# Attention with head mixing, then two MLPs: a times v moved from six visits of a row group to two, and the second mixing moved ahead in the slot behind a visit

## The chip, the cores and the metric

The kernel runs on one core of a Trainium2 chip. The metric is the device time of one execution in microseconds (us); the median of several runs counts.

## The reference, cut to what matters

The kernel computes attention with two mixings over the heads, and then two MLPs on its output. The change is in the attention alone. There are 4 batches of 12 heads, 448 positions and 64 columns a head.

```
scores = scale * q @ k.T                                  # per batch and head, 448 x 448
scores = einsum('bhij,hg->bgij', scores, w_pre)           # first mixing over the heads
attn   = exp(scores - max) / (sum + 1e-9)                 # softmax over j
attn   = einsum('bhij,hg->bgij', attn, w_post)            # second mixing over the heads
out    = attn @ v                                         # "a times v"
x = out as [1792, 768];  x = ((x @ w1) * (x @ w2)) @ w3 @ w_out
x = relu(x @ w_in) ** 2 @ w_out2
```

## The kernel before, in words

**Row groups and blocks.** The 448 rows of a batch are cut in groups of 110, 110, 110 and 118 rows, so there are 16 row groups (s = 0 to 15). A group is cut into blocks of 10 rows times 12 heads, 120 partitions: 11 blocks, or 12 in the fourth group. `BLK` lists all 180 blocks, `first[s]` is the first block of group s.

**The slots.** The loop over `u` (line 1320) runs through 180 slots and six more, one a block. All instructions are put down by hand in this order, and each engine works through its own part of them in that order. In slot u:
- TensorE does the first mixing (`premix`, line 284, two matmul records each) of blocks u + 1 and u + 2 if u is odd, the second mixing (`postmix`, line 380, 12 matmuls) of block u - 4 (`LAG`), and at the end of the slot what is planned for it under `END`: scores (`qk`, line 241) and a times v (`av`, line 494).
- DVE (VectorE) does the row maximum of block u (line 298), every second slot the reciprocals, the low half of the split of E for even blocks (`EL`, line 367), and the low half of the second mixing's output of block u - 5 (`ATl`, line 402).
- ACT (ScalarE) does the high half of that output (`ATh`, line 396) first, then what is planned as `FIRST` (the copy of scores, `evict_s`, line 248, and the copy out of a times v, `put_xh`, line 513), then the exponential of block u (line 306).
- POOL (GpSimd) does the high half of the split of E (`EH`, line 353) and both steps of its low half for odd blocks (`F` and `EL`, lines 364 and 365).
- SP issues the regroup of block u + 5 (`Bt<-S`), after everything else of the slot.

**Work planned by slot.** The dictionary `events` holds, by slot, what comes beside the blocks, each with a kind that says where in the slot it stands (`LOAD`, `FIRST`, `MID`, `LOW`, `END`). A slot with scores or a times v is called a visit here. For group s the scores of the six pairs of heads are made in six visits (`qs`), at the offsets 0, 1, 3, 5, 7, 9 (0, 2, 4, 6, 8, 10 for a long group) from four slots before the first block of group s - 1. Each is six matmuls with 64 rows, in three pairs that run side by side on the two halves of the rows.

A times v of group s comes when all of the group's blocks have passed the second mixing. For each pair p of the six pairs of heads it has two parts of 12 matmuls with 64 output columns, pairs of which run side by side on the two halves of the columns. Before, line 597 finds the six visits of scores that come after group s is done, and puts one pair of heads into each, behind the scores there (line 605). Where there are not six such visits (the last groups), the offsets 0, 1, 3, 5, 6, 7 are used. Three pairs (`hg` 0 or 1) share one accumulator bank (`ps_a`, a pool of one); behind the third, ACT and DVE copy it out as two halves (`put_xh`, `put_xl`, one slot later), and SP stores these (`store_x`, another slot later). The last group is done apart, in pieces between slot 177 and the end.

**Banks.** First mixings have three PSUM banks, second mixings two, the scores one pair of banks, a times v one. A second mixing can start once ATl of the mixing two before has read its bank, and a first mixing once the exponential three blocks before has.

**Other planned work.** In three batches k and v are split into halves while the blocks run: `split_k` on DVE and `split_kl` on POOL every second slot from `ks` on (slots in `full` have ACT make EH of odd blocks instead of POOL); `split_v` on ACT two slots, `split_vl` on DVE one slot ahead of the a times v that needs them. `scale_v` finds the scale of v through two tiny matmuls, whose output lies in the bank of the previous group's a times v (line 445).

Of the kernel before, what the change touches and what calls it, by code (L numbers as in the profile page):

```python
# [18 lines left out]
P = 128  # L19
CP = 112  # L20
F64_BIAS = 2.0 ** -112
NR = 10
ROWS = (110, 110, 110, 118)
LEAD = 5
LAG = 4
EG = 7
EW = 66
TB = 4
# [6 lines left out]
def talking_heads_attention_moe_moe2(  # L35
# [16 lines left out]
    B, _, NDC, S = k.shape  # L52
# [38 lines left out]
    def psum(pool, tag, dt=F32):  # L91
        return pool.tile([P, 512], dt, tag=tag, name=tag)
# [346 lines left out]
    def scale_v(b, i):  # L439

        m = vsum[b]
        if i == 0:
            nc.vector.tensor_reduce(m[:CP, 6:7], m[:CP, 0:6], axis=AX.X, op=ALU.max)
        elif i == 1:
            t = pav[4 * b - 1, 1] if b else psum(ps_a, "a")
            vps[b] = pt = t[:, 512 - P :]
            nc.tensor.transpose(pt[:1, :CP], m[:CP, 6:7], ident[:CP, :CP])
        elif i == 2:
            nc.vector.tensor_reduce(m[:1, 7:8], vps[b][:1, :CP], axis=AX.X, op=ALU.max)
        elif i == 3:  # L450
            nc.tensor.matmul(vps[b][:, :1], ones[:1], m[:1, 7:8], start=True, stop=True)
        else:
            up, lo = pow2(vps.pop(b)[:, :1], 14, "vs")
            nc.vector.tensor_scalar(
                xs[:, b : b + 1], lo, wunscale, 2.0 ** XSH, op0=ALU.mult, op1=ALU.mult
            )
            Vsc[b] = up
# [91 lines left out]
    def at(slot, kind, f, *a):  # L549
        events.setdefault(slot, []).append((kind, len(events), f, a))  # L550

    low_k, crowded, copies = set(), set(), []
    for s in range(2, NSUP):
        b = SUP[s][0]
        base = first[s - 1]
        L = first[s] - base
        qs = [base - 4 + p * L // NDC for p in range(NDC)]
        made = list(qs)
        if s == 2:
            made[:3] = base - 5, base - 2, base - 1  # L560
        for p in range(NDC):
            at(made[p], END, qk, s, p)
            copies.append((base - 2 if s == 2 and p == 0 else made[p] + 1, s, p))
            if p % 3 == 0:
                at(qs[p] - 9, LOAD, load_q, s, p // 3)
                at(qs[p] - 5, MID, split_q, s, p // 3, None)
                if p == 0 and qs[p] - 4 in low_k:
                    crowded.add(qs[p] - 3)
                at(qs[p] - 4 + (qs[p] - 3 in crowded), LOW, split_ql, s, p // 3)
        if s % 4 == 0:  # L570
            ks = [(first[s - 2] + 4) // 2 * 2 + 2 * p for p in range(NDC)]
            full.update(range(ks[0], ks[-1] + 4))
            for p in range(NDC):
                assert ks[p] + 1 < qs[p]
                at(ks[p], MID, split_k, b, p, None)
                at(ks[p] + 1, LOW, split_kl, b, p)
                low_k.add(ks[p] + 1)
                at(ks[p] - 4, LOAD, load_k, b, p)
    for slot, s, p in copies:
        at(slot, MID if slot in crowded else FIRST, evict_s, s, p)  # L580
    for b in range(B):
        f = first[4 * b]
        for i, slot in ((0, 9), (2, 11), (4, 13)):
            at(f + slot, MID, scale_v, b, i)
        for hg in range(2):
            for i in range(3):
                if b or hg:
# [2 lines left out]
                if b == B - 1:  # L590
                    at(f + 3 * hg + i + 13, MID, split_v, b, hg, i)
                    at(f + 3 * hg + i + 14, LOW, split_vl, b, hg, i)
    qk_at = sorted(x for x in events if any(e[2] is qk for e in events[x]))
    for s in range(NSUP - 1):
        for p in range(NDC):
            lo = first[s + 1] + LAG + 1
            at_qk = [x for x in qk_at if lo <= x < lo + SUP[s + 1][3]]
            slot = at_qk[p] if len(at_qk) == NDC else lo + (0, 1, 3, 5, 6, 7)[p]
            if s % 4 == 0 and s < NSUP - 4:
                b = SUP[s][0]  # L600
                assert slot - 2 > first[s] + 13
                at(slot - 2, MID, split_v, b, *divmod(p, 3))
                at(slot - 1, LOW, split_vl, b, *divmod(p, 3))
            for part in range(2):
                at(slot, END, av, s, p, part)
            if p % 3 == 2:
                at(slot + 1, FIRST, put_xh, s, p // 3)
                at(slot + 1, MID, put_xl, s, p // 3)
                if s < NSUP - 2:
                    at(slot + 2, END, store_x, s, p // 3)  # L610

    for b in range(B):
        for i, slot in ((1, 10), (3, 12)):
            at(first[4 * b] + slot, END, scale_v, b, i)

    last = NSUP - 1
    for p in range(NDC):
        for part in range(2):
            at(first[last] + TB + LAG + 1 + (2 * p + part) * (NB - first[last] - TB) // 12,
               END, av, last, p, part, (0, TB * NR))  # L620


    order = ExitStack()
# [693 lines left out]

    mlp_start = first[NSUP - 1] - 4
    early = iter(())
    for u in range(NB + LAG + 2):  # L1320
        if u == NB - LEAD:
            limit[0] = len(chunks)
# [20 lines left out]
        do(LOAD)  # L1343
        if 0 <= u - LAG - 1 < NB - LAG:
            at_h(u - LAG - 1)
        if u in AHEAD:
            postmix(u - LAG)
        if u % 2:
            for x in (u + 1, u + 2):
# [14 lines left out]
                split_l(u - 2)  # L1364
        if 0 <= u - 3 < NB and not low_on_pool(u - 3):
            split_l(u - 3)
        if 0 <= u - LAG < NB and u not in AHEAD:
            postmix(u - LAG)
        if 0 <= u - LAG - 1 < NB - LAG:
            at_l(u - LAG - 1)  # L1370
# [1 line left out]
        do(LOW)  # L1372
        for eng, cost, f in islice(early, STEPS.get(u, 0)):
            f()
        do(END)
        if NB <= u < NB + LAG:
            assert next(early, None) is None
            allow[0] = place["w1", 2]
# [928 lines left out]
```

## Time and profile before

| | us |
|---|---|
| median of 3 runs (lowest, highest) | 1222.35 (1222.11, 1223.85) |
| the profiled execution | 1222.48 |
| its span, first to last instruction | 1220.8 |
| its mean granted TensorE clock | 1.000 |

Mean duration of one instruction, from the page's costliest groups: the row maximum (line 298) 0.612 us, the exponential (line 306) 0.645, ATh (line 396) 0.562, ATl (line 402) 0.645, EL on DVE (line 367) 0.921, EH on POOL (line 353) 0.751, EL on POOL (line 365) 1.162, one record of a first mixing (line 284) 0.560.

How to read it: times are of one profiled execution. A matmul's duration holds its way through the array, and matmuls overlap; what one costs the engine is the distance from its start to the start of the next. A row of the timeline has the start, the duration, the engine, the line, what is written and read, the shape and how many instructions it stands for; a bracket at its end is idle time of the engine before it and what ended it.

### The profile page before, as it was taken

The page shows a single profiled execution, that of the slowest core. Times are in us where ns is not written, and L with a number is a line of the kernel's source. Part 1 is how long each engine was busy: PE and PEld are TensorE (multiplying, and loading weights), DVE is VectorE, ACT ScalarE, POOL GpSimd, SP SyncE. Part 2 cuts the span into 40 slices and gives each one's busy share as a digit, 9 for nine tenths or more (in the row PEclk, how much of TensorE's full clock was granted, in tenths as well). Part 3 has the DMA queues.
Part 4 walks back from the last instruction along what each step waited for, and adds up shares of the span by engine and source line. Part 5 has one row for each costly group of instructions (what it writes and reads, how often), then busy time and mean ns, then how long its engine had stood idle before and what let it go on. Part 6 is the DMA issues. An engine that isn't in the chain of part 4 may idle for free.

```text
span 1220.8 us, 26222 instructions
## 1 busy us (share of the span) xinstructions
PE 1206.9 (99%) x9904; PEld 746.7 (61%) x9904; DVE 948.8 (78%) x1690; ACT 804.5 (66%) x1620; POOL 587.6 (48%) x569
## 2 busy tenths in 40 slices
PE   8999999999999999999999999999999999999998
PEld 3666676676676665555557985555555555666665
DVE  6988899888889956766675876697778775999773
ACT  6887888878888735654464545567878876654430
POOL 3898788889879510110001311446233424666340
PEclk9999999999999999999999999999999999999999
DMA  6466555655645843755543537344478659656562
GB/s 193 129 161 163 138 146 132 171 126 155 172 119 162 242 128 95 175 127 156 134 134 112 189 120 242 127 159 166 160 251 290 240 185 314 207 162 187 171 196 79
DMA packets 139843, 205.02 MB, mean 168 GB/s; under 512 B 33764, under 2 KB 114788, under 8 KB 139716
## 3 DMA queue, kind: packets, MB, share of 16 engines
q1 hardware_dynamic: 136020, 200.01, 55.4%
q10 hardware_dynamic: 3136, 2.40, 0.8%
q8 instruction: 78, 1.28, 0.4%
q0 software_dynamic: 560, 0.93, 0.4%
q14 instruction: 49, 0.40, 0.1%
HBM read 114.60 MB, written 50.16 MB: 135 GB/s over the span
## 4 chain that ended last, share of the span: by engine, by line
PE 90%; DMA 4%; DVE 3%; ACT 1%; issue 0%; SPq 0%; ACTq 0%; POOL 0%
PE mm L1248 25%; PE mm L2113 16%; PE mm L1861 16%; PE p L284 9%; PE o L380 7%; PE mm L1525 5%; PE s L241 5%; PE a L494 4%; DMA Bt<-S 2%; PE p L1248 2%; DVE ATl L402 1%; DMA x<-x_d 1%; DVE EL L367 1%; DVE st L298 1%; ACT E L306 0%; DMA vraw<-in_v_dram 0%
## 5 line engine op out<-in xcount | busy, mean ns | idle before, releaser
L1248 PE MATMUL mm<-x,w 128*128 128x448 f16 x1044 | 197.7, 352 | 0.0
L1248 PEld LDWEIGHTS <-w 128*128 128x128 f16 x1152 | 112.2, 98 | 105.2 <-issue 1.0
L1861 PE MATMUL mm<-x,wq 128*128 128x448 f16 x882 | 169.2, 352 | 0.0
L284 PE MATMUL p<-Bt,wpre_k 120*120 120x448 f32 x360 | 159.4, 560 | 5.7 <-DMA Bt<-S 3.1
L2113 PEld LDWEIGHTS <-ao 128*128 128x128 f16 x1176 | 115.0, 98 | 76.0
L380 PEld LDWEIGHTS <-EH 120*112 120x112 f16 (+1 forms) x1440 | 124.3, 130 | 44.6 <-issue 37.2
L353 POOL TENSOR_SCALAR EH<-E,st 120x448 f16<-120x448 f32 (+1 forms) x152 | 113.0, 751 | 47.7 <-DVE st L336 35.6
L1861 PEld LDWEIGHTS <-wq 128*128 128x128 f16 x882 | 86.0, 98 | 79.6
L402 DVE TENSOR_TENSOR ATl<-o,ATh 112x480 f16<-112x480 f32 x180 | 116.1, 645 | 23.9 <-ACT ATh L396 22.9
L396 ACT CAST ATh<-o 112x480 f16<-112x480 f32 x180 | 101.2, 562 | 45.7 <-PE o L380 40.7
L306 ACT ACTIVATE E<-p,st 120x448 f32<-120x448 f32 x180 | 116.1, 645 | 21.5 <-DVE st L298 13.1
L380 PE MATMUL o<-wph,EH 120*112 120x120 f16 x720 | 124.1, 219 | 1.2 <-DVE ATl L402 1.1
L380 PE MATMUL o<-wph,EL 120*112 120x120 f16 x720 | 122.0, 216 | 0.0
L380 PE MATMUL o<-wpl,EH 120*112 120x120 f16 x720 | 122.0, 216 | 0.0
L365 POOL TENSOR_TENSOR EL<-F,EH 120x448 f16<-120x448 f32 (+1 forms) x90 | 104.6, 1162 | 33.7 <-issue 20.4
L298 DVE TENSOR_REDUCE st<-p 120x1 f32<-120x448 f32 x180 | 110.2, 612 | 2.6 <-PE p L284 2.4
L1248 PE MATMUL mm<-h,M 128*128 128x448 f16 x576 | 110.2, 353 | 0.0
L2113 PE MATMUL mm<-x,ao 128*128 128x384 f16 x588 | 96.5, 326 | 0.0
L2113 PE MATMUL mm<-ow,ao 128*128 128x384 f16 x588 | 96.0, 326 | 0.0
L380 PEld LDWEIGHTS <-EL 120*112 120x112 f16 x720 | 93.6, 130 | 0.0
L367 DVE SCALAR_TENSOR_TENSOR EL<-E,st,EH 120x448 f16<-120x448 f32 (+1 forms) x90 | 82.9, 921 | 10.3 <-POOL EH L353 9.9
L1248 PEld LDWEIGHTS <-M 128*128 128x128 f16 x576 | 55.9, 98 | 52.0 <-DVE M L1435 0.8
(264 smaller groups left out, 2535.1 us busy)
## 6 DMA issues: line engine op xcount, KB each, us to landing
Bt<-S SPq DMA_DIRECT2D x176, 210.0 KB
raw<-in_moe_w_out_dram SPq DMA_DIRECT2D x24, 768.0 KB
g<-ev SPq DMA_DIRECT2D x64, 224.0 KB
gt<-g SPq DMA_DIRECT2D x56, 256.0 KB
raw<-in_moe_w_in_dram SPq DMA_DIRECT2D x16, 768.0 KB
raw<-in_moe_w_dram SPq DMA_DIRECT2D x14, 768.0 KB
raw<-in_moe_w_dram SPq DMA_DIRECT2D x16, 512.0 KB
kept_out<-xa SPq DMA_DIRECT2D x16, 384.0 KB
```

The costliest lines, as they stand in the source:

```text
L284: nc.tensor.matmul(pt[: n * H, :S], wpre_k.rearrange("p t g -> p (t g)")[: n * H, : n * H], Bt.pop(u)[: n * H], start=True, stop=True,)
L298: nc.vector.tensor_reduce(nsum[u][:n, 0, j : j + 1], Pp[u][:n, :S], axis=AX.X, op=ALU.max, negate=True)
L306: nc.scalar.activation(e[:n], Pp.pop(u)[:n, :S].rearrange("p (a b) -> p a b", a=EG), AF.Exp, bias=t[:n, 0, j : j + 1], scale=1.0, accum_ou ...
L353: nc.gpsimd.tensor_scalar(seven(EH[u][:n]), Ex[u][:n], inverse(u), 1.0, op0=ALU.mult, op1=ALU.mult)
L365: nc.gpsimd.tensor_tensor(a, f, b, op=ALU.subtract)
L367: nc.vector.scalar_tensor_tensor(a, e, inverse(u), b, op0=ALU.mult, op1=ALU.subtract)
L380: nc.tensor.matmul(pt[:CP, c * n : (c + 1) * n], a[:n, c * CP : (c + 1) * CP], w[:n, :n], start=(i == 0), stop=(i == 2),)
L396: nc.scalar.copy(ATs[s][0][:, :, :, m * NR : m * NR + nr], src)
L402: nc.vector.tensor_tensor(ATs[s][1][:, :, :, a], src, ATs[s][0][:, :, :, a], op=ALU.subtract)
L1248: nc.tensor.matmul(pt[:, :S], w[a][:, cs], x[z][:, sl], start=(c == 0 and i == 0), stop=(c == len(parts) - 1 and i == 2),)
L1861: nc.tensor.matmul(pt[:, :S], w[:, a, c * P : (c + 1) * P], xop(t, b, kb, c), start=(start and c == 0 and m == 0), stop=(c == 2 and m == 2 ...
L2113: nc.tensor.matmul(pt[:, :OH], y[:, a, q * P : (q + 1) * P], ow[g, q][kb][:, w], start=(start and q == 0 and m == 0), stop=(q == NQ - 1 an ...
```

## The change

A times v of groups 0 to 12 is put into two visits of scores instead of six: three pairs (`hg` 0) at the first visit, three (`hg` 1) at the fourth visit of group s + 3's scores, behind these scores (`END + 1`). Groups 13 and 14, which have no scores to go with, use the offsets 3 and 7. In a slot that follows a visit, the second mixing is issued ahead of the first mixings instead of behind them (`turned`). With it go some shifts: the splits of v stay one a slot and end two slots ahead of the run that needs them, the splits of k begin two slots earlier, `scale_v` has a bank of its own and goes one slot earlier for batches 1 to 3, and the kinds `END + 1` and `END + 2` order scores, a times v and the rest within the end of a slot.

```diff
@@ scale_v
         elif i == 1:
-            t = pav[4 * b - 1, 1] if b else psum(ps_a, "a")
-            vps[b] = pt = t[:, 512 - P :]
+            vps[b] = pt = psum(ps_a, "a")[:, 512 - P :]
@@ the planned work
+    double, from_pool = {}, {}
     for s in range(2, NSUP):
...
-        qs = [base - 4 + p * L // NDC for p in range(NDC)]
-        made = list(qs)
         if s == 2:
-            made[:3] = base - 5, base - 2, base - 1
+            qs = [base - 4 + p * L // NDC for p in range(NDC)]
+            made = [base - 5, base - 2, base - 1] + qs[3:]
+        else:
+            qs = made = [base - 4 + p * L // NDC for p in range(NDC)]
+            double[s] = qs[0], qs[3]
...
-            ks = [(first[s - 2] + 4) // 2 * 2 + 2 * p for p in range(NDC)]
+            ks = [(first[s - 2] + 2) // 2 * 2 + 2 * p for p in range(NDC)]
...
         for i, slot in ((0, 9), (2, 11), (4, 13)):
-            at(f + slot, MID, scale_v, b, i)
+            at(f + slot - (b > 0), MID, scale_v, b, i)
...
-    qk_at = sorted(x for x in events if any(e[2] is qk for e in events[x]))
     for s in range(NSUP - 1):
+        b, lo = SUP[s][0], first[s + 1] + LAG + 1
         for p in range(NDC):
-            lo = first[s + 1] + LAG + 1
-            at_qk = [x for x in qk_at if lo <= x < lo + SUP[s + 1][3]]
-            slot = at_qk[p] if len(at_qk) == NDC else lo + (0, 1, 3, 5, 6, 7)[p]
+            hg, i = divmod(p, 3)
+            slot = double[s + 3][hg] if s + 3 in double else lo + (3, 7)[hg]
             if s % 4 == 0 and s < NSUP - 4:
-                b = SUP[s][0]
-                assert slot - 2 > first[s] + 13
-                at(slot - 2, MID, split_v, b, *divmod(p, 3))
-                at(slot - 1, LOW, split_vl, b, *divmod(p, 3))
+                assert slot - 4 > first[s] + 13
+                at(slot - 4 + i, MID, split_v, b, hg, i)
+                at(slot - 3 + i, LOW, split_vl, b, hg, i)
             for part in range(2):
-                at(slot, END, av, s, p, part)
-            if p % 3 == 2:
-                at(slot + 1, FIRST, put_xh, s, p // 3)
-                at(slot + 1, MID, put_xl, s, p // 3)
+                at(slot, END + 1, av, s, p, part)
+            if i == 2:
+                at(slot + 1, FIRST, put_xh, s, hg)
+                at(slot + 1, MID, put_xl, s, hg)
                 if s < NSUP - 2:
-                    at(slot + 2, END, store_x, s, p // 3)
+                    at(slot + 2, END + 2, store_x, s, hg)
...
-            at(first[4 * b] + slot, END, scale_v, b, i)
+            at(first[4 * b] + slot - (b > 0), END + 2, scale_v, b, i)
...
-               END, av, last, p, part, (0, TB * NR))
+               END + 1, av, last, p, part, (0, TB * NR))
@@ the loop over the slots
+    turned = {x for x in events if any(y[2] in (qk, av) for y in events[x])}
...
-        if u in AHEAD:
+        if u in AHEAD or u - 1 in turned and 0 <= u - LAG < NB:
             postmix(u - LAG)
         if u % 2:
             for x in (u + 1, u + 2):
                 if x < NB:
                     premix(x)
...
-        if 0 <= u - LAG < NB and u not in AHEAD:
+        if 0 <= u - LAG < NB and u not in AHEAD and u - 1 not in turned:
             postmix(u - LAG)
...
-        do(END)
+        for kind in range(END, END + 3):
+            do(kind)
```

## Rows read from the trace of the kernel before

**Rows 1.** The page: busy time, share of the span and instructions of each engine.
```profile
PE 1206.9 (99%) x9904; PEld 746.7 (61%) x9904; DVE 948.8 (78%) x1690; ACT 804.5 (66%) x1620; POOL 587.6 (48%) x569
```

**Rows 2.** Windows: length, busy PE, PEld, DVE, ACT, POOL; clock, DMA share, GB/s.
```profile
260.00:285.00 25.00, 25.00 (x324) 17.23 (x323) 23.25 (x48) 21.67 (x48) 23.76 (x25) 1.00 0.57 149
...
360.00:385.00 25.00, 24.59 (x330) 17.31 (x330) 24.15 (x50) 20.95 (x45) 21.09 (x21) 1.00 0.60 169
...
408.00:430.00 22.00, 19.43 (x356) 14.63 (x355) 20.18 (x49) 16.80 (x37) 12.93 (x16) 1.00 0.97 277
```

**Rows 3.** Timeline, TensorE, two slots with one visit: start, duration, what.
```profile
289.27 0.22 PE L380 MATMUL o<-wph,EH 120*112 120x120 f16 x1
...
290.51 0.37 PE L241 MATMUL s<-kh,ql 64*110 64x448 f32 x2
...
290.81 0.24 PE L494 MATMUL a<-ATh,Vh 112*64 112x110 f16 x2
...
290.93 0.21 PE L494 MATMUL a<-ATh,Vl 112*64 112x110 f16 x2
...
291.37 0.21 PE L494 MATMUL a<-ATh,Vl 112*64 112x110 f16 x2
...
291.51 0.26 PE L380 MATMUL o<-wph,EH 120*112 120x120 f16 x1
...
292.13 0.22 PE L380 MATMUL o<-wph,EL 120*112 120x120 f16 x1
...
292.19 1.72 PE L284 MATMUL p<-Bt,wpre_k 120*120 120x448 f32 x4
...
293.74 0.22 PE L380 MATMUL o<-wph,EH 120*112 120x120 f16 x1
```

**Rows 4.** Timeline, TensorE, an early visit that has scores alone.
```profile
38.12 0.37 PE L241 MATMUL s<-kh,ql 64*110 64x448 f32 x2
38.43 0.26 PE L380 MATMUL o<-wph,EH 120*112 120x120 f16 x1
```

**Rows 5.** Timeline, TensorE, a times v alone between two second mixings.
```profile
396.60 0.22 PE L380 MATMUL o<-wph,EL 120*112 120x120 f16 x1
396.75 0.24 PE L494 MATMUL a<-ATh,Vh 112*64 112x110 f16 x2
...
397.45 0.26 PE L380 MATMUL o<-wph,EH 120*112 120x120 f16 x1
397.55 0.22 PE L380 MATMUL o<-wpl,EH 120*112 120x120 f16 x1
```

**Rows 6.** Timeline, TensorE: first mixings right behind a times v.
```profile
205.01 1.76 PE L284 MATMUL p<-Bt,wpre_k 120*120 120x448 f32 x4
```

**Rows 7.** Timeline, TensorE and DVE, slot 177 in the tail of the stage.
```profile
418.82 0.66 DVE L402 TENSOR_TENSOR ATl<-o,ATh 112x480 f16<-112x480 f32 x1 [0.70 <-ACT ATh L396]
...
420.38 1.99 PE L284 MATMUL p<-Bt,wpre_k 120*120 120x448 f32 x4 [0.85 <-ACT w L890]
...
422.20 0.22 PE L380 MATMUL o<-wph,EH 120*112 120x120 f16 x1
```

**Rows 8.** Timeline, other engines: copies of ACT, an F of POOL, an EL of DVE.
```profile
275.55 1.15 POOL L364 TENSOR_SCALAR F<-E,st 120x448 f32<-120x448 f32 x1
...
289.05 1.05 DVE L367 SCALAR_TENSOR_TENSOR EL<-E,st,EH 120x448 f16<-120x448 f32 x1 [1.11 <-POOL EH L353]
...
295.37 0.91 ACT L248 COPY S<-s 110x896 f32<-110x896 f32 x1 [0.23 <-PE s L241]
...
296.17 0.45 ACT L513 ACTIVATE xt<-a 128x330 f16<-128x330 f32 x1
```

**Rows 9.** Waits, 40 to 430 us: who waited for whom, us, times, longest.
```profile
DVE xt L522 <- ACT xt L513: 9.6, 15, 0.9
...
PE o L380 <- DVE ATl L402: 1.1, 3, 0.5
```

## The prediction, made before the change was run

> **What bounds the kernel now.** The page comes first: TensorE is busy 1206.9 of 1220.8 us [rows 1]. So the time is what TensorE does plus its few waits, and the change touches only the attention stage, some 450 us long. I then read that stage by windows [rows 2]. PE is full or nearly so in the first two of them, and after 408 us it loses 2.6 of 22 us to waits. The granted clock is 1.00 in each, the full one of its two levels (2.4 GHz), so no time is to be had from it. And the other engines are not far behind: DVE at 93 and 97%, ACT at 87 and 84%, POOL at 95% where v is split (260 to 285 us).
>
> Read closer, TensorE keeps a strict rhythm [rows 3]. A times v (line 494) steps by 0.049 us from one pair of matmuls to the next, second mixings (line 380) by 0.053 us from one to the next ((292.13 - 291.51) / 11 is 0.056 with a slow first step). Each change between shapes that use the array differently costs extra: from the third pair of scores to a times v 290.51 to 290.81, 0.30 us; from the last pair of a times v to the mixing 0.14, where 0.049 is the pace. Between second and first mixing nothing extra is paid: 292.13 to 292.19.
>
> **Fewer runs of a times v.** Before, each pair of heads makes its own run behind its own scores, six for each of 15 row groups (the last group is made in pieces). In [rows 3] a run lasts from 290.81 to 291.51, 0.70 us. Its inner pace is (291.37 - 290.93) / 9 = 0.049 us, so its 12 steps alone are 0.587 us, and 0.115 us is entering and leaving. What stands behind the scores does not matter: in [rows 4] scores without a times v reach a second mixing in 0.31 us (38.12 to 38.43), about what they pay to reach a times v. So a visit that loses its a times v saves 0.70 us, the run that receives it grows by 0.587, and 0.115 us is gained for each run that vanishes.
>
> How many vanish: row groups 0 to 12 have scores to follow (s + 3 up to 15), and six runs become two, 4 x 13 = 52: 6.0 us. Groups 13 and 14 have no scores beside them, but for the first visit of 13. A run alone between two second mixings [rows 5] costs 0.15 instead of 0.053 us to enter (396.60 to 396.75), 0.70 for itself (to 397.45), and 0.045 in the first step behind it (0.10 instead of 0.053): less 0.587 that is 0.255 us. Group 13 loses three such and one behind scores; group 14 loses two, since in its other slots the last group's a times v stands anyway. That is 5 x 0.255 + 0.115 = 1.4 us. Sum on TensorE: 7.4 us.
>
> **Second mixing first.** In a slot behind a visit the mixing now stands ahead of the two first mixings. The order itself costs TensorE nothing: the extra of the first step behind a times v is 0.045 us for either (a mixing 0.10 against 0.053 [rows 5]; the four matmuls of the first mixings span 1.76 us behind a times v [rows 6] and 1.72 behind a mixing [rows 3]), and between the mixings nothing is paid. One new neighbour arises, first mixing ahead of scores, about six times. No row shows it; the bounds are nothing and another 0.1 us, like the mixing's way to a times v in [rows 5], 0.6 us in all. I take nothing, since a full-array shape precedes the scores either way.
>
> What the order gives: ACT gets its cast of a mixing (line 396) 1.55 us earlier in an odd slot (292.19 to 293.74 [rows 3]) after a long visit. In the tail there is a measurable piece. The first mixing of slot 177 waits 0.85 us until 420.38 for ACT, which is held up by a weight cast, and the mixing of that slot comes after it, at 422.20 [rows 7]. It now stands ahead and fills 0.63 us of that hole. It can: the ATl that frees its bank ends at 419.48 (418.82 + 0.66 [rows 7]), and its EL was made by POOL a slot before that. I take 0.6 us, between nothing and 0.85.
>
> **What moves on the other queues.** The count of instructions and DMAs is unchanged: store_x still puts two on SP's queue one slot behind each copy out, ahead of that slot's regroup, now at other slots. The splits of v stay one a slot, four to two slots ahead of the run. Those of k (load on SP's queue, copy on DVE, low part on POOL) begin two slots earlier. scale_v gets its own bank and goes one slot earlier, where the previous group's first half has been copied out. None of it is on TensorE's path; I cost it at nothing beside the stalls below, which bound it.
>
> **What the rhythm costs.** This is the unknown. Before, two slots of TensorE last the same each time: from mixing 289.27 to 293.74, 4.47 us [rows 3]. After, two slots with scores alone last 4.47 - 0.70 = 3.77 us and two with a run of three 3.77 + 0.70 + 2 x 0.587 = 5.64 us; up to three of 3.77 follow each other. By their shares in the window of v's split [rows 2] the others need, in two slots, 4.47 x 23.25 / 25 = 4.16 us on DVE, 4.25 on POOL and 3.87 on ACT. A short pair of slots makes POOL fall 0.5 us behind, three of them 1.5; the long pair gives 1.4 back. It fits only just there, and with room elsewhere.
>
> The run also adds a wait. ACT's copy out of a times v (xt, line 513) is queued behind the copy of the scores (0.80 us, 295.37 to 296.17 [rows 8]) and now waits for all three pairs, 0.70 + 2 x 0.587 = 1.87 us from the scores' end. ACT stands for about 1 us, with an exponential and a cast behind it, and DVE's xt behind that, which already waited 9.6 us in 15 such places [rows 9]. One walk, with the means of the page's groups in the table above: scores start at 0, the run ends at 2.65, mixing A at 3.3, two first mixings at 4.85, mixing B at 5.5; then scores, and mixing C at 6.55. C takes A's bank, so A's low part (ATl) must be done by then. ACT: copy of scores to 1.7, xt from 2.8 to 3.1, an exponential to 3.8, at times EH to 4.4, the cast of A to 5.0; DVE's ATl to 5.65. The margin is 0.9 us, so there is no stall where nothing else is full.
>
> It is full in three stretches with v's split, where F takes 1.15 us on POOL [rows 8] and EH, of the same form, 0.75 on average; and in three with k's split DVE waits 1.11 us for POOL's EH ahead of an EL [rows 8]. I charge 0.7 us for each of the first, half of the 1.5 by which POOL falls behind, and 0.35 for each of the second, a third of that wait: 3.2 us. The ends are a gain of 1 us (PE's waits for ATl, 1.1 us in all [rows 9], go) and a loss of 13, below.
>
> The Trainium skill, "SBUF — State Buffer", section "Who interferes with whom", says that GpSimd and a VectorE instruction with two inputs in SBUF shut each other out for a whole instruction. The trace leans that way, as F's 1.15 us shows [rows 8]. By that rule one whole EL, 1.05 us there, could stand before POOL's next step at both runs of a stretch, 2.1 in place of 0.7 us three times: 1221.8, which lies in rival B.
>
> **Sum.** The profiled execution took 1222.48 us (span 1220.8 and 1.7 around it), 0.1 above the median of 1222.35. 1222.5 - 7.4 - 0.6 + 3.2 = 1217.7, against the median 1217.6.
>
> **Rivals.** A: no stall. For it the walk's margin, against it POOL's fill. 1222.4 - 8.0 = 1214.4, or 1213.4 if old waits go too. B: the heavy stretches swallow the gain. About seven of sixteen groups hold a split of k or v; if each loses its 0.46 us and half a microsecond to one more wait, 7 x 0.96 = 6.7 of 8.0 us are gone: 1221. For it POOL at 95% [rows 2]; against it the mean over such a group, 24.1 us of TensorE (4.47 x 5.5 less 0.46) and 23.4 of POOL (4.25 x 5.5). C, slower: ACT's queue decides. If in those seven groups the 0.95 us before xt is never made good, as ACT needs 3.87 us in two slots of 3.77, each of 14 runs costs it: 13.3 - 8.0 = +5, 1227.7. It decides once ATl comes 0.9 us later than in the walk. Against it: the long pair of slots gives ACT 1.8 us. That the change doesn't do what it says is not likely: the runs follow from the slots written out.
>
> **From cases to numbers.** The forecast's own case (1 to 5 us given back, 1215.4 to 1219.8) 0.56, A 0.10, B 0.22, C 0.12. Measurement tells a change from none beyond 0.2%, 2.4 us. Faster, under 1219.9: the forecast and A, 0.66. Same: B, 0.22. Slower: C, 0.12. The range leaves out the far ends of A and C: 1213.5 to 1222.8.
>
> **What would show it.** Runs of 72 matmuls on line 494 behind two of the six scores, each 1.87 us up to the mixing; scores reaching a mixing in 0.30 us; and PE's waits in the stage: few, with POOL or ATl before them in the v stretches if I am right, with ACT's xt before them if C is. PE should be through with the stage 5 us earlier. I am wrong if an added pair takes more than 0.59 us, or if PE waits over 5 us more between 50 and 408 us than before.

## The result, and the profile after

The changed kernel takes 1230.76 us (median of 4 runs, 1230.45 to 1233.65) against 1222.97 for the kernel before beside it: ratio 1.0069, 95% interval 1.0051 to 1.0086. It is slower by 7.8 us. Forecast were 1217.6 us, and the range ended at 1222.8.

The loss lies in the attention stage alone. The second mixing of the last block starts at 441.93 us before and at 450.02 after, and from there to the end of the span it is 778.8 and 779.0 us. Lines have moved: a times v is line 493 now, ACT's copy out 512, DVE's 521, the splits of v 465 and 472; 241, 248, 284, 306, 353, 364 to 367, 380, 396 and 402 are the same. The page: the row that answers to [rows 1], the shares of the chain of work that ended last, by engine, and one of the costliest groups (busy and mean, then the idle time before it and what ended most of it):

```profile
PE 1205.6 (98%) x9904; PEld 741.6 (60%) x9904; DVE 948.5 (77%) x1690; ACT 804.6 (65%) x1620; POOL 590.2 (48%) x569
...
PE 83%; DVE 8%; ACT 3%; DMA 3%; issue 1%; POOL 1%; SPq 0%; POOLq 0%; DVEq 0%
...
L380 PE MATMUL o<-wph,EH 120*112 120x120 f16 x720 | 127.4, 221 | 9.8 <-DVE ATl L402 8.5
```

The same chain and group before:

```profile
PE 90%; DMA 4%; DVE 3%; ACT 1%; issue 0%; SPq 0%; ACTq 0%; POOL 0%
...
L380 PE MATMUL o<-wph,EH 120*112 120x120 f16 x720 | 124.1, 219 | 1.2 <-DVE ATl L402 1.1
```

DVE's share of the chain is the news: 8% in place of 3, while TensorE's fell from 90 to 83%. The windows that answer to [rows 2], and one more:

```profile
260.00:285.00 25.00, 24.37 (x288) 15.91 (x288) 23.27 (x48) 20.82 (x46) 21.09 (x22) 1.00 0.53 137
360.00:385.00 25.00, 24.50 (x325) 16.94 (x323) 22.63 (x51) 21.07 (x47) 21.55 (x22) 1.00 0.54 143
408.00:430.00 22.00, 19.23 (x298) 14.44 (x297) 19.76 (x46) 17.31 (x41) 13.17 (x17) 1.00 0.90 246
185.00:210.00 25.00, 21.89 (x308) 15.45 (x307) 19.90 (x43) 18.30 (x41) 19.08 (x21) 1.00 0.52 133
```

In the last, where k is split, TensorE is idle for 3.1 of 25 us, and every other engine is less busy than TensorE: nothing is full on average, engines wait for each other in turn. Before, TensorE showed no idle time there:

```profile
185.00:210.00 25.00, 25.00 (x333) 17.72 (x333) 23.43 (x49) 20.89 (x47) 21.08 (x25) 1.00 0.54 137
```

TensorE's own work shrank as forecast. A run, from the third pair of scores to the mixing behind it:

```profile
297.61 0.38 PE L241 MATMUL s<-kh,ql 64*110 64x448 f32 x2
297.92 0.24 PE L493 MATMUL a<-ATh,Vh 112*64 112x110 f16 x2
...
299.79 0.26 PE L380 MATMUL o<-wph,EH 120*112 120x120 f16 x1
```

From its first matmul to that mixing it lasts 1.87 us (297.92 to 299.79), the forecast length. Waits I count as the time by which a step of TensorE from one record to the next exceeds its usual pitch, summed from 45 to 430 us. They were 6.0 us before and are 21.5 after. The stage is 8.1 us longer, so 15.5 - 8.1 = 7.4 us of TensorE's work are gone. The 21.5 us are mainly of two kinds.

**The exponential: 9.4 us** (6.7 at the wait and 2.7 in slower steps right behind, 26 places). TensorE, ACT and DVE after a visit with scores alone:

```profile
61.30 0.37 PE L241 MATMUL s<-kh,ql 64*118 64x448 f32 x2
...
61.60 0.26 PE L380 MATMUL o<-wph,EH 120*112 120x120 f16 x1
...
61.71 0.91 ACT L248 COPY S<-s 118x896 f32<-118x896 f32 x1 [1.00 <-PE s L241]
...
62.27 2.03 PE L284 MATMUL p<-Bt,wpre_k 120*120 120x448 f32 x4
...
62.51 0.64 ACT L306 ACTIVATE E<-p,st 120x448 f32<-120x448 f32 x1
...
63.29 0.28 PEld L284 LDWEIGHTS p<-Bt,wpre_k 120*120 120x120 f32 x2 [0.78 <-ACT E L306]
...
64.14 0.22 PE L380 MATMUL o<-wph,EH 120*112 120x120 f16 x1
```

The four records of the first mixings span 2.03 us instead of 1.72 [rows 3]: the second of the two waits for the bank that the exponential three blocks before frees. The exponential is queued on ACT behind the copy of the scores. ACT stands idle for 1.00 us until the scores are there, copies for 0.80 and then needs 0.6 for the exponential, until about 63.1. TensorE has only the mixing and one first mixing to do meanwhile. Before, the a times v behind the scores filled 0.70 us [rows 3], and ACT's two instructions fitted in. The places bear this out: 24 of the 26 lie right behind a visit with scores alone, two in the tail, and none behind one of the 21 visits with a run. In the list of waits below the copy of the scores has 3.3 us and the exponential 26.7: only the order of the rows shows that the copy stands ahead of the exponential.

**ATl: 10.6 us** (14 places, half of them between 1.0 and 1.2 us). POOL, then DVE, then TensorE, around a mixing that waits:

```profile
303.83 1.43 POOL L226 TENSOR_TENSOR ql<-qraw,qh 128x330 fp32r<-128x330 f32 x1
305.22 1.14 POOL L196 TENSOR_TENSOR kl<-kraw,kh 128x448 fp32r<-128x448 f32 x1
306.33 0.65 POOL L353 TENSOR_SCALAR EH<-E,st 120x448 f16<-120x448 f32 x1
```

```profile
307.01 1.05 DVE L367 SCALAR_TENSOR_TENSOR EL<-E,st,EH 120x448 f16<-120x448 f32 x1 [1.96 <-POOL EH L353]
307.98 0.65 DVE L402 TENSOR_TENSOR ATl<-o,ATh 112x480 f16<-112x480 f32 x1
```

```profile
308.68 0.21 PE L380 MATMUL o<-wph,EH 120*112 120x120 f16 x1 [1.02 <-DVE ATl L402]
```

POOL works without a gap through two low halves and EH; DVE's EL waits 1.96 us for that EH, ATl stands behind EL on DVE, and the mixing waits for ATl. The same chain stood in the kernel before, at the same place of the batch (POOL, DVE, TensorE):

```profile
295.52 1.52 POOL L226 TENSOR_TENSOR ql<-qraw,qh 128x330 fp32r<-128x330 f32 x1
297.00 1.13 POOL L196 TENSOR_TENSOR kl<-kraw,kh 128x448 fp32r<-128x448 f32 x1
298.11 0.64 POOL L353 TENSOR_SCALAR EH<-E,st 120x448 f16<-120x448 f32 x1
```

```profile
298.79 1.05 DVE L367 SCALAR_TENSOR_TENSOR EL<-E,st,EH 120x448 f16<-120x448 f32 x1 [1.10 <-POOL EH L353]
299.76 0.64 DVE L402 TENSOR_TENSOR ATl<-o,ATh 112x480 f16<-112x480 f32 x1
```

```profile
300.46 0.21 PE L380 MATMUL o<-wph,EH 120*112 120x120 f16 x1
```

There the EL waited 1.10 us and the mixing was 0.05 us late, since a times v filled 0.70 us ahead of it. A wait that DVE could afford before is one that TensorE pays for now. The waits of after, 40 to 430 us, answer to [rows 9] (who waited for whom: us, times, longest; PEld is the weight load and runs ahead of PE, so not all of its wait is lost: of the 26.7 us, 6.7 show as waits of TensorE):

```profile
PEld p L284 <- ACT E L306: 26.7, 42, 1.4
DVE xt L521 <- ACT xt L512: 19.4, 21, 1.9
...
ACT xt L512 <- PE a L493: 17.6, 22, 1.3
...
DVE EL L367 <- POOL EH L353: 12.4, 12, 2.0
...
PE o L380 <- DVE ATl L402: 8.5, 12, 1.1
...
PEld p L284 <- ACT S L248: 3.3, 17, 0.2
```

and in the kernel before, beside the two of [rows 9]:

```profile
PEld p L284 <- ACT E L306: 15.0, 38, 0.9
...
DVE EL L367 <- POOL EH L353: 8.8, 9, 1.1
ACT S L248 <- PE s L241: 6.8, 29, 0.3
```

ACT's xt does wait for the runs, 17.6 us in all, as the prediction had it; whether that is what TensorE pays for, the trace alone can't say.

### The profile page after: what moved, and what is told of

It reads as the page before. It is cut to its first block, busy times and chain, and to the rows that moved or that the text cites. A ratio compares the mean times of both kernels' runs of the same rounds, so it can differ in the third digit from the quotient of the medians.

```text
span 1229.0 us, 26252 instructions
## 1 busy us (share of the span) xinstructions
PE 1205.6 (98%) x9904; PEld 741.6 (60%) x9904; DVE 948.5 (77%) x1690; ACT 804.6 (65%) x1620; POOL 590.2 (48%) x569
## 4 chain that ended last, share of the span: by engine, by line
PE 83%; DVE 8%; ACT 3%; DMA 3%; issue 1%; POOL 1%; SPq 0%; POOLq 0%; DVEq 0%
PE mm L1248 25%; PE mm L2115 16%; PE mm L1863 16%; PE p L284 6%; PE o L380 6%; PE mm L1527 5%; PE a L493 4%; PE s L241 3%; DVE ATl L402 2%; DMA Bt<-S 2%; DVE EL L367 2%; PE p L1248 2%; DVE st L298 2%; ACT E L306 2%; DVE Vl L472 1%
## 5 line engine op out<-in xcount | busy, mean ns | idle before, releaser
L284 PE MATMUL p<-Bt,wpre_k 120*120 120x448 f32 x360 | 162.8, 560 | 6.9 <-DMA Bt<-S 4.3
L380 PE MATMUL o<-wph,EH 120*112 120x120 f16 x720 | 127.4, 221 | 9.8 <-DVE ATl L402 8.5
L402 DVE TENSOR_TENSOR ATl<-o,ATh 112x480 f16<-112x480 f32 x180 | 115.8, 644 | 13.9 <-ACT ATh L396 12.5
L365 POOL TENSOR_TENSOR EL<-F,EH 120x448 f16<-120x448 f32 (+1 forms) x90 | 98.5, 1095 | 38.2 <-issue 23.6
L396 ACT CAST ATh<-o 112x480 f16<-112x480 f32 x180 | 101.5, 564 | 12.2 <-PE o L380 10.6
L367 DVE SCALAR_TENSOR_TENSOR EL<-E,st,EH 120x448 f16<-120x448 f32 (+1 forms) x90 | 82.9, 921 | 13.9 <-POOL EH L353 13.6
L248 ACT COPY S<-s 110x896 f32<-110x896 f32 (+1 forms) x88 | 80.4, 914 | 17.7 <-PE s L241 15.4
```

The costliest lines, as they stand in the source:

```text
L284: nc.tensor.matmul(pt[: n * H, :S], wpre_k.rearrange("p t g -> p (t g)")[: n * H, : n * H], Bt.pop(u)[: n * H], start=True, stop=True,)
L365: nc.gpsimd.tensor_tensor(a, f, b, op=ALU.subtract)
L367: nc.vector.scalar_tensor_tensor(a, e, inverse(u), b, op0=ALU.mult, op1=ALU.subtract)
L380: nc.tensor.matmul(pt[:CP, c * n : (c + 1) * n], a[:n, c * CP : (c + 1) * CP], w[:n, :n], start=(i == 0), stop=(i == 2),)
L396: nc.scalar.copy(ATs[s][0][:, :, :, m * NR : m * NR + nr], src)
L402: nc.vector.tensor_tensor(ATs[s][1][:, :, :, a], src, ATs[s][0][:, :, :, a], op=ALU.subtract)
```

## The experiments

Times are ratios to the kernel before on the same chip, with 95% intervals; "the changed kernel" is the one above, at 1.0069. Where an expectation names a theory by letter or number, it says what it claims. Four mattered: T1, the copy out of a run on ACT's queue (rival C); T3, the turned order; load, that the splits and low halves on POOL and DVE are too much for the short slots (T2; T4 where k's splits alone are meant); and T5, which I formed only after the first runs, that a times v had covered ACT's copy of the scores.

**Each part alone.** e1 takes the turned order out of the changed kernel, e2 puts it alone into the kernel before.

```diff
-    turned = {x for x in events if any(y[2] in (qk, av) for y in events[x])}
+    turned = set()
```

> The changed kernel with the second mixing put back behind the first mixings everywhere; a times v stays in runs of three. Three theories of the 15.5 us by which TensorE's waits in the attention stage grew (6.0 to 21.5 us between 45 and 430 us): T1, the wait of ACT and DVE for the copy out behind a run of three (17.6 and 19.4 us of their time); T2, the uneven rhythm: pairs of slots that hold scores alone are now shorter (3.77 us) than ACT, DVE and POOL can follow, whatever the copy out does; T3, the order: the first mixings come 0.63 us later in a slot behind a visit, and the maxima and exponentials with them. T1: 1230 to 1234 us. T2: 1228 to 1234 us. T3: 1218 to 1222 us, the 7.4 us of saved changes without the waits.

> The kernel before with the second mixing first in the slot behind a visit, and nothing else of the change; six runs of a times v a row group. T1 and T2: within 1.5 us of before, 1221.5 to 1224.5. T3: 1230 us or more.

e1: 1232.66 us, 1.0087 [1.0070, 1.0104], 22.6 us of waits. e2: 1223.12 us, 1.0001 [0.9989, 1.0012]. Both lie where T1 and T2 put them, and T3 is out: the order costs nothing by itself and is not the cause. What is left of the change is the cause: the runs and the shifts that go with them.

**The copy out one slot later** (e3, in the changed kernel):

```diff
-                at(slot + 1, FIRST, put_xh, s, hg)
-                at(slot + 1, MID, put_xl, s, hg)
+                at(slot + 2, FIRST, put_xh, s, hg)
+                at(slot + 2, MID, put_xl, s, hg)
```

> The changed kernel with the copy out of a times v (ACT's high half, DVE's low half and the stores) one slot later, so that neither ACT nor DVE stands in front of it while the run of three is under way. T1: most of the 15.5 us of waits go, 1217 to 1221 us. T2 and T3: 1228 to 1232 us, though ACT's and DVE's own waits for the copy out fall from 17.6 and 19.4 us to under 5.

1239.45 us, 1.0144 [1.0128, 1.0159]: slower still, and outside both ranges. Its waits, 40 to 430 us:

```profile
ACT ATh L396 <- PE o L380: 26.8, 33, 1.4
PEld p L284 <- ACT E L306: 25.0, 31, 2.4
...
DVE xt L521 <- ACT xt L512: 9.4, 8, 1.4
...
PE o L380 <- DVE ATl L402: 8.6, 14, 1.3
```

ACT's wait for the runs is gone from the list and DVE's xt waits half as long, but TensorE's two kinds of wait are still there, 22.1 us in all against 20.0. T1 falls as the cause of them: ACT's wait in front of xt was there, but TensorE's waits did not go with it. Most of the rest of the 8.7 us over the changed kernel is the later copy itself and the tail: a matmul of scale_v waited 1.37 us for DVE's xt at two places, and in the tail TensorE stood 3.0 us for ACT's EH, up to 431.20, with a mean granted clock of 0.66 from 430 to 440 us, part of it at the lower of its two levels (1.00 in the changed kernel).

**Shorter runs** (e4): the six pairs in four visits, 2, 1, 2, 1.

```diff
-            double[s] = qs[0], qs[3]
+            double[s] = qs
...
+            qv = double.get(s + 3)
+            slot = (qv[0], qv[3])[hg] if qv else lo + (3, 7)[hg]
+            if qv and i == 2:
+                slot = (qv[2], qv[4])[hg]
```

> The changed kernel with a times v of groups 0 to 12 in four visits (two pairs, one, two, one at the scores' first, third, fourth and fifth visit), so two runs a group vanish instead of four (26 x 0.115 = 3.0 us in place of 6.0), and the copy out follows a run of one pair; scale_v takes its place in the bank of the previous group's first half. T1: the waits of before, less 3 to 4.4 us: 1218.5 to 1221 us. T2: short pairs of slots are rarer and are followed by longer ones sooner, about half of the added waits: 1223 to 1228 us. T3: 1229 us or more.

1233.10 us, 1.0092 [1.0077, 1.0107], some 20 us of waits, slower than T1 or T2 forecast (T3's range, but e2 has put T3 out). Halving the runs that vanish does not halve the waits. Visits without a times v remain, two a group in place of four; that these suffice is argued and not shown: by the list of waits the weight loads' wait for the exponential fell from 26.7 to 22.3 us, and the mixings' wait for ATl did not (8.5 and 9.1).

**The splits of k.** e5 gives the changed kernel the old slots of the split, e6 the kernel before the new ones (one line, + 2 against + 4; e5's edit is shown, e6's is its reverse). The slots in which ACT makes EH of odd blocks move with them:

```diff
-            ks = [(first[s - 2] + 2) // 2 * 2 + 2 * p for p in range(NDC)]
+            ks = [(first[s - 2] + 4) // 2 * 2 + 2 * p for p in range(NDC)]
```

> The changed kernel with the splits of k in their old slots (two later). So far the order alone cost nothing (1223.1), runs without it cost 1232.7, the copy out a slot later 1239.5, shorter runs 1233.1, so T1 and T3 in their plain form are out. T2, starvation and short pairs: TensorE gives nothing to ACT, DVE and POOL for as long as a long visit lasts, and these, loaded at 80 to 95%, cannot catch up in the short pairs that follow, most of all where k is split. T4: the splits of k at their new place collide with the visits (the group from 180 to 210 us alone lost 5.8 us). T2: 1228 to 1233 us. T4: 1220 to 1225 us.

> The kernel before with the splits of k two slots earlier, and nothing else of the change. T2: within 2 us of before, 1220.5 to 1224.5. T4: 1227 us or more.

e5: 1229.33 us, 1.0062 [1.0042, 1.0082], in T2's range, and against 1.0069 no difference that the intervals allow to tell. e6: 1227.56 us, 1.0045 [1.0030, 1.0060], in T4's range; its waits are 10.9 us, 3.5 of them in group 6, and those for ATl grow from 1.8 to 4.3. So the shift, which the prediction cost at nothing, costs 5.6 us alone, but given back to the changed kernel it returns about 1 (spans of 1228.0 and 1229.0 us). So the two costs don't add. That both are lateness of the same chain would explain it; no run shows it.

**Less work on DVE and POOL.** e7 (changed) and e8 (before) write only 4 of the 7 parts of EL and F and 2 of the 4 chunks of ATl; the high halves stand in for what is not written, and TensorE's matmuls are the same in number and shape.

```diff
+        e = e[:, :4]
...
-            ATs[s][1][:, :, :, a], src, ATs[s][0][:, :, :, a], op=ALU.subtract
+            ATs[s][1][:, :2, :, a], src[:, :2], ATs[s][0][:, :2, :, a], op=ALU.subtract
```

> The changed kernel with less work beside TensorE: EL is made for 4 of 7 parts of its columns only (on DVE and POOL, F too), ATl for 2 of 4 chunks, and TensorE reads the high halves in place of the parts left out, so its own matmuls are the same in number and shape. DVE loses about 1 us in two slots, POOL 0.7. T2: the waits go, and this is the changed kernel's TensorE time: 1213 to 1217 us, 4 to 8 us under the kernel before with the same relief. If the added waits are of another kind (the copy out, DMAs, SP's queue), it stays at 1226 us or more.

> The kernel before with the same relief, as a control. T2 and T4: its waits outside the tail are 3 us, so 1218 to 1222 us. If TensorE were slowed by something that the relief removes from its own stream, it would fall further.

e7: 1223.03 us, 1.0007 [0.9998, 1.0016]; e8: 1218.87 us, 0.9969 [0.9959, 0.9980]. e8 came as forecast; e7 fell between its two forecasts, so neither holds alone. The waits are 14.8 us against 3.1. In e7 ATl's fall from 10.6 to 2.5 us, those around the exponential stay: 6.5 and 3.2. So load makes the one kind and not the other, and with it gone the change still costs 4.2 us: 11.7 us more of waits, less the 7.4 saved. T5 came from here.

**Which engine makes ATl late.** e17 relieves DVE alone (its EL and ATl), e18 POOL alone (F and EL).

> The changed kernel with VectorE alone relieved: of ATl it writes 2 of the 4 chunks (the high halves stand in for the rest), of its EL 4 of 7 parts; GpSimd keeps all its EL, and TensorE's matmuls are the same in number and shape. Theory D (the second mixings wait for ATl because VectorE is too full): the waits for ATl fall from 10.6 us to under 4, and the time goes to 1223 to 1226. Rival P (VectorE is late because GpSimd's EL and the release of EH behind it are late): ATl's waits stay above 7 us and the time is 1228 to 1231. By both the waits for the exponential stay at about 9 us.

> The changed kernel with GpSimd alone relieved: its F and EL for the odd blocks write 4 of the 7 parts (high halves stand in for the rest); VectorE keeps all its work, and TensorE's matmuls are the same in number and shape. Theory D (VectorE is too full): ATl's waits stay above 7 us and the time is 1228 to 1231. Rival P (GpSimd's EL is late and VectorE waits for it): ATl's waits fall under 4 us and the time goes to 1223 to 1226. By both the waits for the exponential stay at about 9 us.

e17: 1224.86 us, 1.0026 [1.0016, 1.0035]; e18: 1227.79 us, 1.0046 [1.0029, 1.0063]. ATl's waits are 3.0 and 6.9 us by my count. By the list of waits, e17:

```profile
DVE EL L369 <- POOL EH L353: 13.5, 14, 2.0
...
PE o L382 <- DVE ATl L404: 2.2, 5, 1.0
```

and e18:

```profile
DVE EL L369 <- POOL EH L353: 8.6, 8, 2.0
...
PE o L382 <- DVE ATl L404: 4.7, 9, 1.3
```

e17 came as theory D had it. Rival P falls in its plain form: relieving F and EL on POOL did not bring ATl's waits under 4 us. But theory D missed e18's bounds too, by 0.1 and 0.2 us, and e17 leaves DVE's wait for POOL's EH as it was (13.5 us against 12.4). The chain runs through both engines, EL behind POOL's EH and ATl behind EL, and a relief of either shortens the waits, DVE's by more; the place at 308.68, 1.09 us late, was 0.26 late in e17 and 0.81 in e18. What stands ahead of EH on POOL there, the low halves of q and k, no run shortened.

**Without its cover, in the kernel before** (e14): the scores behind a times v instead of ahead of it, in all visits from group 3 on; no runs.

```diff
-            at(made[p], END, qk, s, p)
+            at(made[p], END + (s > 2), qk, s, p)
...
+        do(END + 1)
```

> The kernel before with a times v ahead of the scores in each visit (groups from the third on), so that nothing of TensorE stands between the scores and the mixings of the next slot. No run of three, the same six visits, the same work in each. T5 (a times v covered ACT's copy of the scores): the second of two first mixings now waits for the exponential behind visits in odd slots, some 40 of them by 0.2 to 0.4 us, 1230 to 1238 us. T2 (starvation in long visits): no long visit, within 2 us of before.

1238.18 us, 1.0133 [1.0120, 1.0147], 0.2 above T5's range and 14 above T2's. Nothing has moved to another slot, and the work is the same; 16 us are lost all the same. Waits, 40 to 430 us:

```profile
ACT S L248 <- PE s L241: 41.1, 59, 1.3
PEld p L284 <- ACT E L306: 34.6, 42, 1.1
```

The waits around the exponential are 12.1 and 3.6 us, where the kernel before has about 1 of each; that is 13.8 of the 13.8 us by which the waits grew (6.0 to 19.8). ACT's wait for the scores was 6.8 us before. With T2's condition absent, this shows T5's mechanism: the a times v behind the scores was the cover for ACT's copy of them.

**Taking the copy out of the exponential's way.** e9 (changed), e10 (before) and e11 (changed with k's old slots) put the copy of the scores behind the exponential in all visits; e12 is e11 with the copy out behind it too; e13 leaves the first visit of each group as it was:

```diff
-        at(slot, MID if slot in crowded else FIRST, evict_s, s, p)
+        at(slot, MID, evict_s, s, p)                                          # e9 to e12
+        at(slot, MID if slot in crowded or s > 2 and p else FIRST, evict_s, s, p)   # e13
```

> The changed kernel with ACT's copy of the scores put behind the exponential of its slot instead of ahead of it, for all visits. The runs so far split the added waits in two: about 9.6 us, in some 30 places of 0.32 us, where the second of two first mixings waits for ACT's exponential (still there, 9.6 us, when DVE and POOL are relieved), and about 10.6 us where the second mixing waits for ATl (gone with the relief but for one group). T5: the first kind is a chain, scores - copy of the scores on ACT (0.80 us) - exponential behind it (0.6) - third bank of the first mixings, against 1.5 us of TensorE's work; a times v behind the scores had covered it. T5: those waits go, 1220 to 1224 us. T2 alone (ACT late because it starved in the run before): the waits stay, 1229 to 1233 us.

> The kernel before with the same move, as a control: there a times v still covers the copy. T5: nothing to win, 1221 to 1224 us. If the copy's place matters for another reason, 1218 us or less, or above 1226.

> The changed kernel with the copy of the scores behind the exponential and the splits of k in their old slots. T5, with the 1.4 us that the old slots gave before: 1218.5 to 1222.5 us, the first chance to beat the kernel before. T2 alone: 1227 to 1231 us.

> As the last one, with ACT's copy out of a times v behind the exponential too. If the wait of ACT for the run of three still costs something once the first chain is gone (T1 in part), 1 to 3 us less than the last one; if not, within 1 us of it, or more, as DVE's low half of the copy out then comes later.

> The changed kernel with ACT's copy of the scores behind the exponential only for pairs 1 to 5 of a group, where the scores after it come two slots later. T5: most of the 9.4 us of waits for the exponential go, those for ATl stay: 1221 to 1226 us. T2 alone: 1229 us or more.

e9: 1237.58 us, 1.0125 [1.0110, 1.0140]; e10: 1234.02, 1.0093 [1.0078, 1.0108]; e11: 1237.92, 1.0123 [1.0108, 1.0138]; e12: 1235.25, 1.0098 [1.0081, 1.0115]; e13: 1232.68, 1.0087 [1.0074, 1.0101]. None gains. e9 and e11 lie above both their ranges, and e10 shows that the copy's place matters by itself: the move costs the kernel before 11.3 us. In e9 the waits around the exponential fall from 9.4 to 5.9 us, but the next scores wait 6.4 us for their banks, which ACT now frees later, and ATl's grow to 12.8. In e13 they fall to 5.9 as well, and ATl's grow from 10.6 to 13.9. T5's figure for e13 (a gain of several us) was wrong, and the time lies where T2 put it: the wait moved. e12 took 2.7 us less than e11, in its range for "T1 in part", though the intervals overlap: the scores' waits for their banks fall from 6.5 to 1.8 us. So with the copy of the scores moved, ACT's wait for a run did cost TensorE something.

**Both at once** (e16): e7 with e13's move.

> Both remedies on the changed kernel: EL for 4 of 7 parts and ATl for 2 of 4 chunks with TensorE's own work unchanged, and the copy of the scores of pairs 1 to 5 behind the exponential. If the two causes are all there is, few waits are left: 1212 to 1217 us, clearly under the kernel before with the relief (1218.9). If something else stands behind both, 1220 us or more.

1217.91 us, 0.9968 [0.9956, 0.9979], between its two forecasts; waits 9.7 us, in groups 1 to 12 only 4.2 (16.1 in the changed kernel); the rest lies in the tail, where TensorE waits for the exponential and for regroups. That is 5 us under e7 but not measurably under e8, the kernel before with the same parts left out. So with DVE and POOL relieved and the copy moved, the change costs nothing, and it still gains nothing: e8 has 6.6 us less of waits, nearly all of the 7.4 saved. e8 has not the move of the copy; a kernel before with both was not run.

**Runs only where they may fit** (e15): the kernel before with runs of three only beside the scores of groups 5, 10, 13 and 15, where k is not split.

```diff
+            if s + 3 in (5, 10, 13, 15):
+                base = first[s + 2]
+                slot = base - 4 + 3 * (p // 3) * (first[s + 3] - base) // NDC
```

> The kernel before with runs of three only behind the scores of row groups 5, 10, 13 and 15, whose later visits lie in even slots (no first mixing waits there for an exponential behind the copy of the scores) and where k is not split; scale_v of the third batch has a bank of its own, one slot earlier. 16 runs vanish, 1.8 us. T5 and T2 together: 1219.5 to 1221.5 us, faster than both kernels by a little. If runs of three cost something in themselves: 1222 to 1225 us.

1223.90 us, 1.0009 [1.0000, 1.0018]: no gain, with 7.7 us of waits. That is not where T5 and T2 together put it but in the range for a cost of the runs themselves. The profiled execution, the slowest of the eleven, holds besides these waits a stop of 1.9 us inside an a times v (from 421.12 us) for which the profile shows no cause, so this run decides little between the two. No version that computes everything beat the kernel before.

## Why the prediction was wrong, point by point

- **What bounds the kernel** (TensorE, other engines not far behind): right, and the second half of it deserved more weight.
- **Fewer runs of a times v**, 7.4 us: right. A run is 1.87 us, scores reach a mixing in 0.30 (61.30 to 61.60), and the sum by the stage's length is 7.4.
- **Second mixing first**: right that it costs nothing (e2). The neighbour taken at nothing, first mixing ahead of scores, costs 0.09 us five times (0.47 instead of 0.376), the upper bound. The 0.6 us in the tail did not come: the hole at slot 177 went, and a mixing there waits for ATl in its place, 1.02 us by pitch:

```profile
426.15 0.21 PE L380 MATMUL o<-wph,EH 120*112 120x120 f16 x1 [0.86 <-DVE ATl L402]
```

- **What moves on the other queues**, "nothing beside the stalls below": wrong for k's split, 5.6 us alone (e6), though about 1 in the changed kernel (e5).
- **What the rhythm costs**: this is the step that failed. 3.2 us were charged, 15.5 measured. With 0.6 for the tail that is the 12.9 us between the sum (4.8 us saved) and the stage (8.1 us lost). It failed in two ways. The walk went through a visit with a run and checked one deadline there, ATl ahead of the mixing two on; in it DVE stood idle until the cast was done. It was not made for a visit with scores alone, where the second of the two first mixings needs the exponential's bank and the copy of the scores stands ahead of that exponential with no a times v to cover it: 9.4 us, 0.3 in most of 26 places. "No stall where nothing else is full" was therefore wrong; groups with no split lost 4.2 us more than before. And the charges for the heavy stretches, 0.7 and 0.35 each, were shares of a lag instead of the chain walked through: the three groups with v's split lost 3.7 us more than before, the three with k's split 7.6, where four mixings of group 6 come 1.0 to 1.2 us late, each behind an EL for which DVE waited 1.12 us for POOL's EH. The row that gave this was there, EL's 1.11 us [rows 8].
- **Rivals.** A's margin did not exist. B had one of the right places (k, POOL, DVE) and less than half the price. C had the sign and, at 1227.7, some of the size, but by luck: ACT waits in front of xt as it says, yet with that wait gone TensorE's two kinds of wait stay (e3), and it showed a cost, 2.7 us, only where the copy of the scores had been moved (e12 against e11).
- **The Trainium skill** ("SBUF — State Buffer", "Who interferes with whom") on GpSimd and a VectorE instruction with two inputs in SBUF: the trace agrees for F. The 48 of 90 that began while DVE's EL ran took 1.00 us or more each, where the median of the 15 that met no EL is 0.64; before, 31 began so. POOL's kl, of one shape and 18 times, took 1.13 to 2.10 us, with a median of 1.50 against 1.14 before; the nine over 1.3 us met no EL, but each met one of DVE's casts of k or q, so they are no case of this rule. POOL's whole busy time moved by only 2.6 us [rows 1]. No run here tried the rule alone, so its part in the waits for ATl stays open.

What stays open: how much of the 4.2 us in the groups without a split comes from each kind of wait, what the new slots of v's split and of scale_v cost, which no run moved by themselves, and whether other slots for k and v would let the runs pay.

## What to carry to other kernels

An engine's work that looks movable may be the cover of another engine's chain: before taking it away, list every buffer that is freed behind the point, and walk each to its deadline with the queue ahead of it, not the tightest one alone. An idle wait on an engine that is not the bound can be stored lateness, as DVE's 1.1 us were here: where slots are made uneven, charge it in full to the short ones. Where one remedy moves a wait instead of ending it, a run that relieves two causes together, with its control, shows what the change was worth at best.

## What the runs showed of the hardware that was not expected

A first mixing that has waited for its bank loses about 0.10 us more in its next step, 0.47 instead of 0.376, behind every wait of this kind in the changed kernel. An F of POOL that began while DVE's EL ran took 1.00 us or more, 48 times of 48, in place of 0.64. The order of two pieces of work on one engine, at equal work, was worth 16 us of 1222 (e14), 13.8 of them as waits for an exponential queued behind a copy.
